# Attention and a routed mixture of experts in one kernel: the end of a batch in fewer VectorE steps at other places, x turned one tile a pair, and a new order of the first and last pairs

## The chip, the cores and the metric

One core of a Trainium2 chip runs the whole program. The metric is device time in microseconds of one execution; lower is better. TensorE (PE) multiplies, VectorE (DVE), ScalarE (ACT) and GpSimd (POOL) do elementwise work, SyncE (SP) starts most transfers.

## The reference, cut to what matters

Attention with a decay, 8 batches of 8 heads, 576 positions of 64 values, and its output `x` (4608 tokens of 512) into a mixture of 8 experts of which each token uses one:

```python
scores = q @ k.T / 8                           # per batch and head, 576 x 576
cum    = cumsum(log(clip(f, 1e-4, 1)))         # decay, per position
scores = where(causal, -1e9, scores + cum[:, None] - cum[None, :])
attn   = exp(scores - max); attn /= sum + 1e-9
x      = (attn @ v)                            # -> 4608 x 512
logits = x @ w_gate                            # 4608 x 8
e      = argmax(logits); g = softmax(logits)[e]
out    = g * (relu(x @ w1[e]) @ w2[e])         # w1 512 x 1024, w2 1024 x 512
```

## The kernel before, in words

**Attention in pairs.** `attention_all` (L183) handles two heads of a batch at a time: 32 pairs, four to a batch, in a loop over n = 0 to 32. The 576 query rows of a head are four tiles of 128 and a short one of 64; the short tiles of both heads are treated together, as "joint rows". In iteration n the scores of pair n are multiplied (L358, joint rows L391), reduced with bias and mask on VectorE (L342, custom operations that add the bias and give the row's largest value), and exponentiated on ScalarE (L377, joint L383). The turned probabilities (64 x 64 turns L410, copied by ScalarE or VectorE at L422; the last rows by L405 and L467) and the products with the values (L481, in two halves AVa and AVb, whose copies to `xT` are `xa` and `xb`) belong to pair n-1.

**What sets the order.** The table `PERIOD` lists each iteration's steps in program order, and `InOrder.pin` makes each engine keep it. Between the steps lie numbered and lettered slots, 0, E, 1, 2, 3, U, X, 4, 5, C, V, F, 6. Slot U is behind VectorE's reduction r12; X is on TensorE between the last turns and the joint rows J; 4 is ahead of the last turns TL and AVa; C is ahead of `xb`; V and F are behind it. Two reductions matter here: `r10` stands behind `tl` (the L467 copy), and the joint reductions `rj0` and `rj1` lie around `xa`.

**Banks.** Turns and products go to seven PSUM banks given out in a cycle (`next_bank`); a bank is free again when its copy has run.

**The end of a batch.** `fin_tasks` (L585) puts tasks into slots of the iterations after a batch's last pair: gate matmuls on TensorE (`fin_gate`, L557), the turning and scaling of x's five row tiles (`fin_x`: turns L410 or L405, products with 1/sum L516 on VectorE, write to DRAM), the logits (`fin_logits`, turns L405, five products L575, sum L581), then the routing of `route_stages` (L819): softmax, expert, gate (L864 to L870), rank (matmuls L875 and L877, sums L882 to L887), slot (L894 to L908), a high one-hot (L912; GpSimd multiplies it by the gate values, L919, Rr), a low one-hot (L926) and the table (matmuls L933, sum L937). Each routing stage is some two to eight VectorE operations on 128 x 5 or 128 x 40; many of their tiles lie in a PSUM bank, `ps_r`. The plan is, as (iterations after, slot): gate matmuls (0, X); x tiles 0 and 1 (0, F); logits (1, X); softmax and expert (1, V); gate (2, U); rank (2, X); slot and high one-hot (2, V); low one-hot (3, U); table (3, X); x tiles 2, 3 (3, F) and 4 (3, C).

**Start and end.** `first_bias` (L248) makes the first pair's bias by products of ones (L255) and copies (L260). q and k are rounded (L293) and what the rounding left is kept as well (`rest`, L298). `selects` (L301) masks a bias tile on GpSimd: joint rows L309, diagonals L314 to L318. In the last pairs expert 0 is begun: three blocks of gathered rows of x are fetched by GpSimd (`fetch`, L1062) in iteration 30, w1's four blocks are loaded and split (L999, L1000), and first up-products run (`up`, L1111), put into slots by the tables of `extra`; `Moe.finish` (L1178) lists the rest of expert 0 and the last batch's routing.

```python
            at("X"), ("J", 0, s_joint), ("r11", 0, most(1, 1)), at(4), ("TL", 1, av_last),
            ("AVa", 1, lambda n: av(n, 0)), ("e11", 0, power(1, 1)), ("tl", 1, out_last),
            ("r10", 0, most(1, 0)), ("e02", 0, power(0, 2)), ("e13", 0, power(1, 3)),
            ("rj0", 0, lambda n: red_joint(n, 0)), ("AVb", 1, lambda n: av(n, 1)), at(5),
            ("xa", 1, lambda n: av_out(n, 0, "v")),
            ("rj1", 0, lambda n: red_joint(n, 1)), ("e12", 0, power(1, 2)), at("C"),
            ("xb", 1, lambda n: av_out(n, 1, "v")), at("V"), at("F"), ("ej", 0, exp_joint), at(6),
```

## Time and profile before

| | us |
|---|---|
| median of 3 runs (lowest, highest) | 800.54 (800.32, 813.82) |
| the profiled execution | 802.31 |
| its span, first to last instruction | 800.6 |
| TensorE busy | 767.2 |
| VectorE busy | 551.1 |
| ScalarE busy | 502.6 |
| GpSimd busy | 500.2 |

The span is the time from the first to the last recorded instruction, and what lies around it in the profiled execution is 1.7 us. The mean granted TensorE clock over the span is 0.981 of full speed. Attention takes about the first 356 us, the experts the rest. How to read it: the chain of waits follows the work that ended last back from the last instruction, and gives for each stretch of time what was running or waited for; the distance between two values products (L481) in that chain is the length of one pair.

### The profile page before, as it was taken

Reading aid. Unit: us, or ns where it says so; the run is one execution under the profiler, and the core shown is the slowest. Engines: PE = TensorE matmul, PEld = TensorE weight load, DVE = VectorE, ACT = ScalarE, POOL = GpSimd, SP = SyncE. Lnnn points to the kernel's source line nnn. Section 1 sums busy time; section 2 is a strip of 40 time slices with the busy share of each in tenths; the row PEclk is TensorE's granted clock in tenths of the full one; section 3 lists DMA queues with packets and bytes.
Section 4 is the critical chain, followed back from the end, with each engine's and each line's share of the span. In section 5 each row is a group of like instructions: output and inputs, shape, how many; then the busy total and the mean of one; then the engine's idle time right before and its main releaser. Section 6 shows DMA issues by size and latency. Waiting matters only on the chain.

```text
span 800.6 us, 18864 instructions
## 1 busy us (share of the span) xinstructions
PE 767.2 (96%) x6640; PEld 640.9 (80%) x6640; DVE 551.1 (69%) x1643; ACT 502.6 (63%) x1276; POOL 500.2 (62%) x620
## 2 busy tenths in 40 slices
PE   5999999999999999989999999999999999999996
PEld 3777776767676767678989899898898898998985
DVE  5668787777888786735388848758478488486630
ACT  5997886887878786755366646456365365463521
POOL 5997685858595957751568657546556475475311
PEclk9999998999999999899999999999999999999999
DMA  7766574847565757421446352363343433523300
GB/s 185 209 170 180 145 218 120 220 135 209 148 206 146 206 149 215 147 89 64 141 110 201 106 165 84 107 197 101 116 144 106 154 93 106 165 74 106 111 26 32
DMA packets 78817, 112.15 MB, mean 140 GB/s; under 512 B 9343, under 2 KB 40063, under 8 KB 78720
## 3 DMA queue, kind: packets, MB, share of 16 engines
q1 hardware_dynamic: 71680, 90.97, 39.6%
q0 software_dynamic: 6400, 19.93, 7.7%
q8 instruction: 54, 0.88, 0.4%
q14 instruction: 43, 0.35, 0.1%
q10 hardware_dynamic: 640, 0.01, 0.0%
HBM read 91.85 MB, written 20.07 MB: 140 GB/s over the span
## 4 chain that ended last, share of the span: by engine, by line
PE 87%; DVE 8%; issue 2%; ACT 1%; DMA 0%; POOL 0%; DVEq 0%; ACTq 0%; POOLq 0%
PE ps L1147 28%; PE ps L1342 19%; PE ps L481 12%; PE ps L358 6%; PE ps L410 6%; PE ps L391 5%; PE ps L1111 4%; DVE sc L342 2%; PE ps L405 2%; PE pr L1342 1%; PE ps L1298 1%; PE ps L557 1%; DVE xT L422 1%; PE pr L933 1%; ACT sc L377 0%
## 5 line engine op out<-in xcount | busy, mean ns | idle before, releaser
L377 ACT ACTIVATE sc<-sc,nmx 128x512 f32<-128x512 f32 (+3 forms) x256 | 142.2, 559 | 24.4 <-DVE nmx L342 24.1
L1147 PE MATMUL ps<-w_0w,hhw 128*128 128x512 f32 x280 | 112.9, 403 | 0.0
L1342 PE MATMUL ps<-X_0w,w1s 128*128 128x320 f32 x504 | 111.7, 309 | 0.0
L422 ACT COPY aT<-ps 128x512 f32<-128x512 f32 (+1 forms) x224 | 94.2, 506 | 27.1 <-PE ps L410 24.2
L1147 PE MATMUL ps<-w_0w,hl 128*128 128x512 f32 x280 | 110.8, 396 | 0.0
L1147 PE MATMUL ps<-w_1w,hhw 128*128 128x512 f32 x280 | 110.4, 394 | 0.0
L1155 POOL DMA_INDIRECT out<-y,si_fast x37 | 37.1, 1004 | 96.8 <-ACT y L1154 88.1
L358 PE MATMUL ps<-hl 64*128 64x512 f32 (+3 forms) x768 | 90.7, 351 | 4.9 <-DVE xT L422 2.6
L481 PE MATMUL ps<-aT,va_t 128*64 128x256 f32 (+3 forms) x896 | 93.7, 361 | 0.3 <-DVE aT L467 0.3
L298 POOL TENSOR_TENSOR hl<-raw,hl 128x512 fp32r<-128x512 f32 (+1 forms) x62 | 83.6, 1349 | 5.0
L1342 PEld LDWEIGHTS ps<-X_0w,w1s 128*128 128x128 f32 x504 | 84.2, 188 | 0.0
L1154 ACT ACTIVATE y<-ps,g_fast 128x512 f32<-128x512 f32 x37 | 25.5, 689 | 87.6 <-PE ps L1147 64.9
L481 PEld LDWEIGHTS ps<-aT,va_t 128*64 128x64 f32 x896 | 57.9, 140 | 27.4 <-issue 2.9
L1342 PE MATMUL ps<-X_1w,w1s 128*128 128x320 f32 x252 | 77.9, 309 | 0.0
L358 PEld LDWEIGHTS ps<-hl 64*128 64x128 f32 x768 | 60.6, 195 | 9.4 <-PE ps L410 3.1
L342 DVE CUSTOM_DVE_ANT_0 sc<-ps,bias 128x128 f32<-128x128 f32 (+1 forms) x128 | 59.2, 481 | 5.8 <-PE ps L358 3.2
L1147 PEld LDWEIGHTS ps<-w_0w,hl 128*128 128x128 f32 x280 | 52.5, 187 | 12.7
L1147 PEld LDWEIGHTS ps<-w_1w,hhw 128*128 128x128 f32 x280 | 52.8, 189 | 11.1
L1389 POOL TENSOR_TENSOR u<-u,u 128x320 f32<-128x320 f32 x27 | 23.6, 876 | 60.7 <-DVE u L1387 60.4
L1147 PEld LDWEIGHTS ps<-w_0w,hhw 128*128 128x128 f32 x280 | 52.5, 188 | 11.0
L342 DVE CUSTOM_DVE_ANT_1 sc<-ps,bias 128x256 f32<-128x256 f32 (+1 forms) x128 | 58.8, 485 | 0.3
L1342 PE MATMUL ps<-xa,w1s 128*128 128x320 f32 x336 | 58.2, 308 | 0.2 <-ACT u L1376 0.2
(241 smaller groups left out, 1886.2 us busy)
## 6 DMA issues: line engine op xcount, KB each, us to landing
bias<-ud SPq DMA_DIRECT2D x31, 576.0 KB
w1r<-in_w SPq DMA_DIRECT2D x112, 128.0 KB
w<-in_w SPq DMA_DIRECT2D x28, 512.0 KB
raw<-in_qkT SPq DMA_DIRECT2D x64, 160.0 KB
raw<-in_qkT SPq DMA_DIRECT2D x64, 144.0 KB
va_t<-in_va SPq DMA_DIRECT2D x32, 256.0 KB
x_dram<-row SPq DMA_DIRECT2D x32, 256.0 KB
wraw<-in_w SPq DMA_DIRECT2D x7, 512.0 KB
```

What stands on the lines that cost most here:

```text
L298: return eng.tensor_tensor(hl[:, 1], raws[n][:, r : r + w], hl[:, 0].bitcast(F32), ALU.subtract)
L342: V.tensor_tensor_reduce(dst, src, in1, -0.125, init, ALU.add, ALU.min, nms[n][:, col : col + 1])
L358: note(nc.tensor.matmul(pb[j][:, o : o + w], hl[js, q, P * t : P * t + P], hl[js, k, 512 : 512 + w], start=(i == 0), stop=(i == 2),))
L377: A.activation(x, x, AF.Exp, bias=nms[n][:, 5 * j + t : 5 * j + t + 1], scale=-1.0, accum_out=ssums[b][:, t, 2 * p + j : 2 * p + j + 1])
L391: note(nc.tensor.matmul(pb[half][64 * j : 64 * j + 64, 0:JW], raw[:, 512 + 64 * j : 576 + 64 * j], raw[:, 640 + JW * half : 640 + JW * hal ...
L410: note(nc.tensor.transpose(out.bitcast(F32R), words, c.identr[rows, rows]))
L422: copy_on = {"a": lambda o, i: A.copy(o, i), "v": lambda o, i: V.tensor_copy(o, i)}
L481: note(nc.tensor.matmul(pv[j * HD : (j + 1) * HD, q0 - qa : qb - qa], l, r, start=(blk == 0), stop=(blk == nb - 1),))
L1111: c.note(nc.tensor.matmul(ph[:, 0:n], w[:, wi, fs], x[xi][:, kt, :], start=(k == 0), stop=(k == 3 * KT - 1),))
L1147: c.note(nc.tensor.matmul(py, rows(hi_, ft), w[wi], start=(ft + k == 0), stop=(ft == FT - 1 and k == 2),))
L1155: nc.gpsimd.indirect_dma_start(out=self.out, out_offset=bass.IndirectOffsetOnAxis(ap=si[:, s : s + 1], axis=0), in_=y, in_offset=None, bou ...
L1342: self.nc.tensor.matmul(bank[:, 0:HN], w[:, wi, mat, kt], x[xi][:, kt, :], start=start and k == 0, stop=k == 5, skip_group_check=True,)
```

## The change

**The batch end.** A tile of x is turned in slot X and written out in slot V, one tile a pair and the last two together (`fin_x` gives two steps; its two half banks are taken at the turning). Logits are turned at X, scaled at 4 with two products in place of five, summed at C. Softmax and expert go to U a pair later, gate to 4 with five of its eight operations on GpSimd, rank to X of the next pair, its sums to 4, slot to C, high one-hot to U, low to C, table to X and its sum to 4 of the pair after. For the batches from 5 on the logits come a pair earlier. The small tiles lie in SBUF instead of `ps_r`; a second subtraction, two memsets, a cast and a sum are dropped. In `PERIOD`, V goes to the place behind `tl`, ahead of `rj0`, and `r10` goes ahead of slot 4.

**The start.** Eleven products of a zero tile run on TensorE ahead of the bias products. `rest` of pair 0 goes ahead of `first_bias`. The second pair's q and k are loaded earlier and rounded ahead of the masks. The joint rows of the first bias are copied from PSUM by ScalarE, and GpSimd masks the diagonals first and then 64 columns of the joint rows alone.

**The end.** The early fetches go from slot 0 to slot 2 of iteration 30, behind the masks of pair 31; w1's blocks are loaded and split in other slots, one of them by ScalarE and VectorE; the first up-products go to slots 3, U, X, 5 and 6 of iteration 32, and `finish` begins with the last batch's logits.

```diff
+        idle = c.words["xT", 0]
+        V.memset(c.values["xT", 1][:, 0:512], 0.0)
+        V.tensor_copy(idle[:, 0:512], c.values["xT", 1][:, 0:512])
+        pi = next_bank()
+        for _ in range(11):
+            note(nc.tensor.matmul(pi, idle[:, 0:P], idle[:, 0:512], start=True, stop=True))
...
+            for c0, w, k in ((512, S - 512, 2), (0, 512, 0)):
+                for j in range(2):
+                    rows = slice(64 * j, 64 * j + 64)
+                    pin(A.copy(biases[0][rows, BJ + c0 : BJ + c0 + w], pb[k + j][rows, 0:w]))
...
+        load_raw(1)
+        for part in (Q, K):
+            pin(rest(0, V, part))
         pin(A.activation(warm, fr[0:1, 0:1], AF.Exp))
         first_bias()
-        for part in (Q, K):
-            pin(rest(0, V, part))
...
-        joint, diagonals = selects(0)
-        joint(384)
+        for part in (K, Q):
+            rounded(1, A.copy, part)
+        diagonals, joint = selects(0)
         diagonals()
-        joint(0, 384)
+        for part in (K, Q):
+            rest(1, G, part)
+        joint()
...
-            at("X"), ("J", 0, s_joint), ("r11", 0, most(1, 1)), at(4), ("TL", 1, av_last),
+            at("X"), ("J", 0, s_joint), ("r11", 0, most(1, 1)),
+            ("r10", 0, most(1, 0)), at(4), ("TL", 1, av_last),
             ("AVa", 1, lambda n: av(n, 0)), ("e11", 0, power(1, 1)), ("tl", 1, out_last),
-            ("r10", 0, most(1, 0)), ("e02", 0, power(0, 2)), ("e13", 0, power(1, 3)),
+            at("V"), ("e02", 0, power(0, 2)), ("e13", 0, power(1, 3)),
...
-            ("xb", 1, lambda n: av_out(n, 1, "v")), at("V"), at("F"), ("ej", 0, exp_joint), at(6),
+            ("xb", 1, lambda n: av_out(n, 1, "v")), at("F"), ("ej", 0, exp_joint), at(6),
...
-            for dn, i, f in [
-                (0, "X", lambda: fin_gate(b)), (0, "F", fx[0]), (0, "F", fx[1]),
-                (1, "X", lg[0]), (1, "X", lg[1]), (1, "V", softmax), (1, "V", expert),
-                (2, "U", gate), (2, "X", rank), (2, "V", slot), (2, "V", hi), (3, "U", lo),
-                (3, "X", table), (3 - 2 * late, "F", fx[2]), (3 - late, "F", fx[3]),
-                (3 - late, "C", fx[4]),
-            ] + after:
+            fx = [fin_x(b, *ts) for ts in ((0,), (1,), (2,), (3, 4))]
+            soon = b >= B - 3
+            k = 1 - soon
+            plan = [(0, "E" if soon else "X", lambda: fin_gate(b))]
+            for i, (f, e) in enumerate(fx):
+                plan += [(i, "X", f), (i, "V", e)]
+            plan += [
+                (k, "X", lg[0]), (k, 4, lg[1]), (k, "C", lg[2]),
+                (k + 1, "U", softmax), (k + 1, "U", expert), (k + 1, 4, gate),
+                (k + 2, "X", rank), (k + 2, 4, ranked), (k + 2, "C", slot),
+                (k + 3, "U", hi), (k + 3, "C", lo),
+            ]
...
+                plan += [(k + 4, "X", table), (k + 4, 4, tabled)]
...
-        w.oh = tokens(80, 6)
-        V.tensor_tensor(w.oh[:, 0:5], bc(w.ei), c.iota5m, ALU.is_equal)
-        V.memset(w.oh[64:128, 4, :], 0.0)
-        V.memset(w.oh[:, 5, :], 0.0)
-        w.ohb = rs.tile([P, 6, E], BF16, name="ohb")
-        V.tensor_copy(w.ohb, w.oh)
+        V.tensor_tensor(c.ohb[:, 0:5], bc(w.ei), c.iota5m, ALU.is_equal)
...
-            V.tensor_copy(vl[:, :, 3 + i], gw)
+            G.tensor_copy(vl[:, :, 3 + i], gw)
             if i < 2:
-                V.tensor_tensor(gw, gw, vl[:, :, 3 + i], ALU.subtract)
+                G.tensor_tensor(gw, gw, vl[:, :, 3 + i], ALU.subtract)
...
-        for kt in range(KT):
+        for kt in (0, 3, 1, 2):
...
-        return [(4, "V", self.early_index)] + [
-            (5, 0, lambda m=m: self.fetch(0, m)) for m in range(NA)
+        return [(4, "C", self.early_index)] + [
+            (5, 2, lambda m=m: self.fetch(0, m)) for m in range(NA)
...
-        return {0: [up(0)], "E": [out, up(1)], 1: [out], 4: [up(2), out],
-                6: [up(3), out, up(4), out]}.get(i, [])
+        return {3: [up(0)], "U": [up(1)], "X": [out], 5: [out], 6: [up(2), out]}.get(i, [])
```

The order of instructions shows it at three places (line, operation, out<-in, shape). First, VectorE in the pair of the gate stage. Before, the stage's eight operations stand between r12, whose largest values are `nmx`, and the copy of turns to `aT`:

```order
L864 TENSOR_REDUCE pr<-ex 128x5
L865 TENSOR_SCALAR pr<-pr 128x5
L866 RECIPROCAL pr<-pr 128x5
L868 CAST vals<-pr 128x5
L870 TENSOR_TENSOR pr<-pr,vals 128x5
L868 CAST vals<-pr 128x5
L870 TENSOR_TENSOR pr<-pr,vals 128x5
L868 CAST vals<-pr 128x5
L422 COPY aT_91<-ps 128x4x64
L342 ISA sc_02_73,nmx<-ps,bias 128x128
L342 ISA nmx 128x1
```

After, the same engine ahead of the last rows' copy (L478) of the pair of the gate stage; L353 is the score reduction:

```order
L353 ISA sc_11_81,nmx<-ps,bias 128x256
L353 ISA nmx 128x1
L353 ISA sc_12_79,nmx<-ps,bias 128x128
L353 ISA nmx 128x1
L908 TENSOR_REDUCE gw<-ex 128x5
L909 TENSOR_SCALAR gw<-gw 128x5
L910 RECIPROCAL gw<-gw 128x5
L478 COPY aT_91<-ps 64x2x64
L533 TENSOR_TENSOR row<-ps,rinv 128x4x64 x2
```

The gate stage is three operations here, in slot 4, and the writing of x (L533, `row`) stands directly behind the L478 copy.

Second, VectorE in the pair that has the slot stage, from the last rows' copy's surroundings on. Before, around both output copies to `xT`, the joint reductions (`sc_J`) come first and the slot stage behind the second copy:

```order
L342 ISA sc_J,nmx<-ps,bias,nmx 128x288
L342 ISA nmx 128x1
L422 COPY xT_83<-ps 128x256
L894 TENSOR_REDUCE r<-rk 128x5
L895 SCALAR_TENSOR_TENSOR key<-pr,r 128x5
L899 TENSOR_TENSOR th<-pr,iotaP 128x20
L904 TENSOR_REDUCE hi<-th 128x5
L906 SCALAR_TENSOR_TENSOR pr<-hi,pr 128x5
L908 SCALAR_TENSOR_TENSOR pr<-pr,hi 128x5
L912 TENSOR_TENSOR eqh<-pr,iotah 128x200
L722 MEMSET ssum 64x8
L342 ISA sc_03_57,nmx<-ps,bias 128x512
```

After, where two tiles of x are written in the same pair:

```order
L478 COPY aT_97<-ps 64x2x64
L533 TENSOR_TENSOR row<-ps,rinv 128x4x64 x2
L533 TENSOR_TENSOR row<-ps,rinv 64x4x64 x2
L353 ISA sc_J,nmx<-ps,bias 128x288
L353 ISA nmx 128x1
L433 COPY xT_83<-ps 128x320
L353 ISA sc_J,nmx<-ps,bias,nmx 128x288
L353 ISA nmx 128x1
L936 SCALAR_TENSOR_TENSOR key<-ei,rkp 128x5
L940 TENSOR_TENSOR th<-rkp,iotaP 128x20
L945 TENSOR_REDUCE hi<-th 128x5
L947 SCALAR_TENSOR_TENSOR lo<-hi,rkp 128x5
```

The four writes stand ahead of the first joint reduction, and the slot stage between the second joint reduction and the second output copy.

Third, GpSimd in iteration 30. Before, the rows of x are fetched (`xg`) and a weight block is split ahead of the mask of the last pair's `bias`:

```order
L298 TENSOR_TENSOR hl<-raw,hl 128x576
L1062 DMA xg<-x_dram,gi_early 128x512 x3
L999 CAST w_6344<-wraw 128x1024
L1000 TENSOR_TENSOR w_6344<-wraw,w_6344 128x1024
L309 AFFINE_SELECT bias<-bias 64x576 x2
L314 AFFINE_SELECT bias<-bias 128x2x128
L316 AFFINE_SELECT bias<-bias 128x2x192
L318 AFFINE_SELECT bias<-bias 128x2x256
L1000 TENSOR_TENSOR w_6462<-wraw,w_6462 128x1024
```

After, the mask stands ahead of the fetch:

```order
L308 TENSOR_TENSOR hl<-raw,hl 128x576
L319 AFFINE_SELECT bias<-bias 64x576 x2
L325 AFFINE_SELECT bias<-bias 128x2x128
L327 AFFINE_SELECT bias<-bias 128x2x192
L329 AFFINE_SELECT bias<-bias 128x2x256
L1105 DMA xg<-x_dram,gi_early 128x512 x3
L912 CAST vals<-gw 128x5
L914 TENSOR_TENSOR gw<-gw,vals 128x5
L912 CAST vals<-gw 128x5
```

The fetches, and the splitting of the weight block, moved behind the four mask rows; the gate stage's GpSimd rows (`vals`, `gw`) follow the fetches.

## Rows read from the trace of the kernel before

**Rows 1.** The first page: busy time of each engine (share of the span, instructions), and the chain of work that ended last, by engine.
```profile
PE 767.2 (96%) x6640; PEld 640.9 (80%) x6640; DVE 551.1 (69%) x1643; ACT 502.6 (63%) x1276; POOL 500.2 (62%) x620
...
PE 87%; DVE 8%; issue 2%; ACT 1%; DMA 0%; POOL 0%; DVEq 0%; ACTq 0%; POOLq 0%
```

**Rows 2.** The chain of waits (start us, us, what) in the stretch from 41 to 52 us, which has no batch end: the values products of two pairs that follow each other.
```profile
41.93 2.87 PE ps L481 x32
...
50.24 1.77 PE ps L481 x17
```

**Rows 3.** Busy time by windows (window: length, then busy us and instructions of PE, PEld, DVE, ACT, POOL, the granted TensorE clock as a share of 2.4 GHz, DMA share, GB/s): ten us of plain pairs, three stretches of the first batches, two whole batches, and a stretch of the last pairs.
```profile
30.00:40.00 10.00, 10.00 (x153) 8.15 (x151) 7.33 (x30) 9.58 (x29) 9.42 (x20) 1.00 0.75 197
77.00:80.40 3.40, 3.17 (x25) 1.79 (x21) 2.70 (x17) 2.20 (x7) 0.00 (x1) 0.50 0.03 11
118.00:124.80 6.80, 6.80 (x51) 4.51 (x52) 4.66 (x28) 5.35 (x16) 1.41 (x1) 0.50 0.31 84
162.70:165.80 3.10, 2.88 (x20) 1.48 (x18) 2.45 (x15) 1.89 (x7) 0.16 (x1) 0.51 0.06 20
187.10:269.10 82.00, 77.54 (x1042) 59.59 (x1042) 66.09 (x286) 66.67 (x207) 59.89 (x89) 1.00 0.61 179
343.40:346.70 3.30, 3.23 (x10) 3.23 (x11) 0.68 (x3) 0.00 (x0) 2.27 (x5) 0.51 0.21 79
```

**Rows 4.** The chain of waits (start us, us, what) through one batch in the middle: five values products, and between them pieces of TensorE and VectorE.
```profile
187.08 2.87 PE ps L481 x32
...
192.74 1.28 PE ps L410 x32
...
194.75 0.55 PE ps L405 x5
...
196.60 2.92 PE ps L481 x32
...
203.90 0.13 DVE pr L864
...
205.55 0.18 PE pr L875
...
205.84 1.12 PE ps L391 x8
...
207.14 2.89 PE ps L481 x32
...
214.31 0.75 DVE Ar L926
...
215.10 0.69 PE pr L933 x5
...
217.09 2.87 PE ps L481 x32
...
225.72 1.11 PE ps L557 x16
...
228.12 2.87 PE ps L481 x32
```

**Rows 5.** VectorE's groups in that batch (201.1 to 242.15 us), shapes of one line together: line, operation, out<-in, shapes, count | busy us, mean ns | idle before.
```profile
L516 DVE TENSOR_TENSOR row<-ps,rinv 128x256 f32<-128x256 f32 (+1 forms) x9 | 3.5, 442 | 1.2 <-PE ps L405 1.2
...
L467 DVE COPY aT<-ps 64x128 f32<-64x128 f32 x4 | 1.1, 280 | 1.3 <-PE ps L405 1.3
...
L887 DVE TENSOR_REDUCE pr<-rk 128x5 f32<-128x40 f32 x1 | 0.2, 203 | 0.0
...
L894 DVE TENSOR_REDUCE r<-rk 128x5 f32<-128x40 f32 x1 | 0.2, 185 | 0.0
```

**Rows 6.** GpSimd's groups in the same stretch, same columns.
```profile
L919 POOL TENSOR_TENSOR Rr<-eqh,vals 128x240 bf16<-128x240 bf16 x5 | 2.8, 586 | 6.8 <-DVE eqh L912 6.8
```

**Rows 7.** The chain of waits in the stretch from 78 to 81 us: the joint rows of pair 6.
```profile
78.42 2.12 PE ps L391 x8
```

**Rows 8.** VectorE's timeline at the start (start us, us, line, operation, out<-in, count, in brackets the idle time before it and what ended it).
```profile
9.69 1.49 DVE L298 TENSOR_TENSOR hl<-raw,hl 128x512 fp32r<-128x512 f32 x2
...
12.63 0.69 DVE L342 CUSTOM_DVE_ANT_0 sc<-ps,bias 128x512 f32<-128x512 f32 x1 [1.33 <-PE ps L358]
...
18.89 0.69 DVE L342 CUSTOM_DVE_ANT_0 sc<-ps,bias 128x512 f32<-128x512 f32 x1 [1.83 <-POOL bias L314]
```

**Rows 9.** GpSimd's timeline at the start, same columns.
```profile
9.68 1.71 POOL L309 TENSOR_SCALAR_AFFINE_SELECT bias<-bias 64x192 f32<-64x192 f32 x2 [7.13 <-ACT bias L260]
```

**Rows 10.** The chain of waits over the last pairs: the values products of pairs 29 to 31 (written in the next pair's steps) and the last one.
```profile
310.19 2.89 PE ps L481 x32
...
323.04 4.45 PE ps L481 x32
...
337.13 2.87 PE ps L481 x32
...
355.93 1.96 PE ps L481 x20
```

**Rows 11.** GpSimd's timeline in the last pairs: the first of three early fetches of rows of x, and the mask of the last pair.
```profile
315.69 1.22 POOL L1062 DMA_INDIRECT xg<-x_dram,gi_early  x1 [4.29 <-DVE row L516]
...
322.85 1.39 POOL L309 TENSOR_SCALAR_AFFINE_SELECT bias<-bias 64x576 f32<-64x576 f32 x2
```

**Rows 12.** TensorE's waits from 300 to 360 us (its line <- the engine, tile and line waited for: us in total, times, longest).
```profile
PE ps L1111 <- DVE xa L1082: 1.5, 1, 1.5
```

More of the change, by code (lines that the diff above doesn't have):

```diff
@@ L320, in diagonals @@
                                 channel_multiplier=1)
-            return joint, diagonals
+            return (joint, diagonals) if n else (diagonals, lambda: joint(512))
         def added(n, j, t):
@@ L583, in attention_all @@
         tasks, later, order = {}, [], InOrder(tc)
         def fin_tasks(b):
-            (softmax, expert, gate, rank, slot, hi, lo, table), after = batch_done(
-                b, lambda: lgs[b][0], next_bank
-            )
-            fx = [lambda t=t: fin_x(b, t) for t in range(5)]
-            lg = [lambda p=p: fin_logits(b, p) for p in range(2)]
+            (softmax, expert, gate, rank, ranked, slot, hi, lo, table, tabled), after = batch_done(
+                b, lambda: lgs[b], next_bank
+            )
@@ L695, in prepare @@
                 load_bias(n + 2)
-            if n == 0 and i == 0:
+            if n == 0 and i == 2:
                 late_consts()
-                for part in (Q, K):
-                    rounded(1, A.copy, part)
-                for part in (Q, K):
-                    rest(1, G, part)
             if n + 1 < NP and i == 1:
@@ L730, in behind @@
                 todo = fin_tasks(b - 1)
-            for f in tasks.pop((n, i), []):
-                step(f)
             if n >= NPAIR:
@@ L739, in behind @@
                     fin_sums(b - 1, part)
+            for f in tasks.pop((n, i), []):
+                step(f)
             if (n, i) == (NP, 0):
@@ L822, in route_stages @@
     V = nc.vector
+    G = V if last else nc.gpsimd
     rs = c.rps
```

221 lines of the change are left out of this document (122 added, 99 removed).

## Prediction

> **What bounds the kernel now.** I read the first page, then the chain of waits pair by pair, then the busy time by windows, then VectorE's groups. TensorE is busy 96% of the 800.6 us span and carries 87% of the chain that ended last; VectorE carries 8% of the chain though it is busy only 69% [rows 1]. So time can be won only where TensorE stands, or turns at half speed, and those places are few.
>
> The ruler is the distance from one pair's values products (L481) to the next. Plain pairs, with no batch-end work, come every 8.31 us (41.93 to 50.24) [rows 2]; in them TensorE is busy 10.00 of 10 us and ScalarE 9.58, so ScalarE is nearly a second bound there [rows 3]. A batch in the middle takes 41.04 us (187.08 to 228.12), in steps of 9.52, 10.54, 9.95 and 11.03 [rows 4]. Four plain pairs are 33.24. TensorE's own batch-end work is: gate 1.11, table 0.69, logits turns 0.55, the rank 0.29 (205.55 to 205.84), and the turns of x. Thirty-two half turns took 1.28, so one is 0.04 and the 32 of x's four full tiles cost 1.28; four whole turns for the short tile are 0.44 by 0.55 for five [rows 4]. The sum is 4.36. So the work is 33.24 + 4.36 = 37.6, and 3.4 us of each batch are waits. The busy time bounds that from the other side: 77.54 of 82.00 us over two batches leaves 2.2 a batch [rows 3].
>
> Where the 3.4 are: take each step, less 8.31 and its own work. Step 1 has logits and two tiles of x (0.55 + 0.64): 0.0 left. Step 2 has the rank: 10.54 - 8.31 - 0.29 = 1.9 left. It is the gate chain: eight small VectorE operations from 203.90 to 205.5, behind which the rank waits, and the joint rows (L391) stand behind the rank on TensorE [rows 4]. Step 3 has the table: 0.95 left, the slot chain and, from 214.31, the low one-hot L926, for which the table at 215.10 waits [rows 4]. Step 4 has gate, two tiles and the short tile: 11.03 - 8.31 - 1.11 - 1.08 = 0.5 left.
>
> **The change in the batch.** TensorE's work stays 4.36; only its place moves. On VectorE the small operations cost about 0.2 us each: 185 ns for one sum over 40, 203 for another [rows 5]. Counting the order rows, a batch end had some 46 VectorE operations and has some 33: five of the gate's eight go to GpSimd, one subtraction, two memsets, a cast and a sum are dropped, the logits' five multiplications become two. That is 13 x 0.19 = 2.5 us less VectorE time a batch. This alone is worth nothing where VectorE is idle. What counts is order:
>
> - The softmax stands where the gate chain stood, but its rank comes a pair later, so nothing stands behind it on TensorE. The 1.9 us of step 2 go.
> - The table comes a pair after the low one-hot, and its sum on VectorE is a slot of its own: the 0.95 of step 3 go.
> - New: the writing out of x (two of 442 ns a tile) stands between the last turns' copy and the first joint reduction, no longer behind the second output copy. Banks go round in sevens. In the logits' pair, the first values product gets the bank that this write must free, and it is asked for before the copy. It then waits for the copy (0.28) and one write (0.44): 0.7 [rows 5].
> - New: the exponential of the softmax sits in ScalarE's queue and waits for two small VectorE operations (0.2 each) and then takes about as long itself, an estimate. Behind it are copies that free banks for the joint rows. ScalarE has 0.4 us of slack in 10 [rows 3], so most shows: 0.5, at most 0.9.
> - New: with the short tile, four writes (1.8 us) and the slot chain (four small ones, 0.8) stand ahead of the second output copy, which the next pair's second group needs a bank from: 0.6.
> - With some 0.3 for the half-microsecond waits that stay, new and old waits are 0.7 + 0.5 + 0.6 + 0.3 = 2.1 where 3.4 were. The batch becomes 39.7: 1.35 us less. Bounds: no new wait shows (-3.4), or the new ones are double (+0.6).
>
> Five GpSimd operations more a batch are hidden: GpSimd stands idle 6.8 us before Rr in that batch anyway [rows 6], and its other work there is for pairs to come. If that cover went, they would cost about 1 us.
>
> Six batch ends lie in the steady stretch: 6 x 1.35 = 8.1 us.
>
> **The clock.** [...] One stretch so costs 1.0 us (at most 1.7, if all of the 3.4 were work); four cost 4.3. With shorter waits some won't come. I can't tell which: I take 2 of 4.3, with 0 and 4.3 as ends.
>
> **The start.** Rounding's remainder of the first pair, 1.49 us for two on VectorE from 9.69, held the first scores until 11.2; it moves ahead of the bias copies, where VectorE stands waiting for the bias products [rows 8]. GpSimd's joint mask (1.71 at 9.68) moves behind the diagonals, so the first score reduction, at 12.63 after a wait of 1.33 for TensorE, can go at about 11.3 [rows 8, 9]. The second pair's reduction at 18.89 had waited 1.83 for a mask on GpSimd [rows 8]; that mask comes about as much earlier, as the joint mask of pair 0 shrinks. Together 1.3 to 2.3 of the path, and I take 2.0. The eleven products of zeros run before 6.8, when TensorE has nothing; they cost nothing if they end by then. By the joint rows' 0.14 to 0.27 us for 288 columns one of 512 is 0.25 to 0.47 (an estimate), eleven are 2.7 to 5.2 us from about 2 on: at the long end they push the bias products back by half a microsecond. Ends: -3 and 0.
>
> **The end.** Here three pairs took 12.85, 14.09 and 18.80 us (310.19, 323.04, 337.13, 355.93) [rows 10]. Ahead of the last mask on GpSimd stood the early fetches, the first of which waited until 315.69, so that the mask began at 322.85 [rows 11]; now it is first and can begin near 311, so that pair 31's reductions stop waiting. The fetch comes after it at little loss: its rows are turned from the end of that pair on. The up-products at 343.4 ran at half clock behind a 1.5 us wait for xa [rows 3, 12]; they now stand later, spread over four slots. Against that, the copy of one w1 block moves to ScalarE and its subtraction to VectorE, where a pair without a batch end leaves room. I take 12.85 to 11.1, 14.09 to 11.5 and 18.80 to 17.2: 1.75 + 2.6 + 1.6 = 6.0; ends 2 (only the mask's step) and 9.
>
> The sum is 8.1 + 2 + 2 + 6 = 18.1. The profiled execution took 802.31 us (1.7 around its span), the median of the runs is 800.54, so I count from the median: 800.5 - 18.1 = 782.4, say **782 us**.
>
> [...] Two rows differ in where the result goes: a sum over 40 into SBUF took 185 ns, the like into PSUM 203 [rows 5]. So moving the small tiles out of PSUM saves some 18 ns an operation, 16 operations, 0.3 us a batch, which I left out. [...]
>
> **Rivals.**
> - *The waits only move.* The values product waits for the write of x, ScalarE for the softmax, and the batch stays near 41. For it: ScalarE's 9.58 of 10 [rows 3], and VectorE's steps in the joint stretch are packed. Against: the gate chain's 1.9 us is the one long wait, and it has no like afterwards. Then only start, end and a little clock remain: 2 + 6 + 1, so 791 us.
> - *All waits go.* No new wait shows: 6 x 3.4 = 20.4, clock 4.3, start 2, end 8: 35 less, 766 us. Against: three named waits each have a queue behind them.
> [...]
> - *It doesn't do what it says* at the ends: the zeros delay the bias products and the fetch comes late for its turns. 8 less is won: 790, within the first rival's range.
>
> **How the numbers follow.** Forecast 0.56 (its own range 777 to 788), waits only move or ends fail 0.30, all waits go 0.09, clock oftener 0.05. The range of 8 in 10 cuts the last two partly: 772 to 794. A change of 2%, 16 us, is about what a measurement of this kernel can tell from none, so faster means below 784.5: seven tenths of the forecast's 0.56 (0.39), all of 0.09, and a tenth of 0.30, with the unknown end's luck 0.55; slower than 816.5 only the worst of the last rival and what I have not seen, 0.04; the rest, 0.41, is the same.
>
> **What would show it.** Right: values products of a middle batch 39.7 us apart over four pairs, the step of the rank under 9.5, no VectorE chain ahead of L391, the chain's share of VectorE below 8%, first scores near 9, last pairs near 11, 11.5 and 17. Wrong: TensorE waiting over 1 us a batch for the write of x or for copies behind the softmax's exponential; half-clock stretches in every batch; the first score reduction still after 12 us; the last pairs as long as before.

## The result, and the profile after

| | before | changed |
|---|---|---|
| median of 4 runs, us | 800.43 | 778.99 |
| lowest and highest | 796.13, 813.82 | 777.24, 780.01 |
| profiled execution: span, mean granted clock | 800.6, 0.981 | 778.2, 0.987 |

The ratio is 0.9747, with a 95% interval of 0.9701 to 0.9793: faster by 2.5%. The forecast was 782 us. Runs of a kernel that took over 1.5% longer than its fastest one at a lower granted clock are left out of every ratio, but not of the medians.

The first page after, busy times and the chain by engine:

```profile
PE 756.6 (97%) x6679; PEld 639.5 (82%) x6679; DVE 545.5 (70%) x1546; ACT 504.5 (65%) x1280; POOL 508.0 (65%) x655
...
PE 88%; DVE 5%; ACT 3%; issue 2%; POOL 1%; DMA 1%; SPq 0%; ACTq 0%; POOLq 0%; DVEq 0%
```

Against [rows 1], TensorE's share rose to 97%, and VectorE's part of the chain fell from 8% to 5%. VectorE's busy time fell by only 5.6 us (551.1 to 545.5), where eight batches of the forecast 2.5 us would be 20; the last section shows why. So VectorE's total doesn't explain the gain; what it is made of, the runs below take apart.

The chain of waits through one batch in the middle (start us, us, what; L492 are the values products, L973 the table, L416 whole turns, L919 the rank, L402 the joint rows, L421 half turns, L891 the softmax's subtraction):

```profile
135.68 2.87 PE ps L492 x32
...
142.67 0.62 PE pr L973 x5
...
143.72 0.55 PE ps L416 x5
...
145.59 0.74 issue
146.33 2.94 PE ps L492 x32
...
152.72 0.21 DVE sh L891
...
152.96 0.02 ACT ex L895
...
153.10 1.40 ACT aT L433 x4
...
155.43 2.87 PE ps L492 x32
...
162.43 0.53 PE ps L421 x16
162.95 0.13 PE pr L919
...
163.19 1.12 PE ps L402 x8
...
164.49 2.87 PE ps L492 x32
...
174.47 2.87 PE ps L492 x32
```

The batch takes 38.79 us (135.68 to 174.47) where 41.04 were [rows 4], in steps of 10.65, 9.10, 9.06 and 9.98. The rank at 162.95 runs without a wait, and the joint rows follow at once. Two waits are new, and both were foretold: 0.74 us of "issue" at 145.59, ahead of the values products in the logits' step, and the softmax's exponential at 152.96, which starts only when VectorE's subtraction (L891, to 152.93) is done, with four copies of ScalarE (1.40) behind it, for which the joint rows wait.

Values products over the last pairs, those of [rows 10]:

```profile
293.41 2.94 PE ps L492 x32
...
302.68 2.87 PE ps L492 x32
...
314.02 2.94 PE ps L492 x32
...
329.85 2.87 PE ps L492 x32
```

The three steps are 9.27, 11.34 and 15.83 us. Before, they were 12.85, 14.09 and 17.4. The last of these is not the 18.80 of the prediction: the row at 355.93 in [rows 10] has 20 of the pair's 32 products, and TensorE's timeline of before shows the first twelve earlier:

```profile
354.46 1.20 PE L481 MATMUL ps<-aT,va_t 128*64 128x320 f32 x12
355.93 1.84 PE L481 MATMUL ps<-aT,va_t 128*64 128x256 f32 x16 [0.27 <-DVE aT L467]
```

So the chain's distance is the length of a pair only between rows that both hold all 32; from here on, steps go by a pair's first product.

Windows (length, busy us and instructions of PE, PEld, DVE, ACT, POOL, granted TensorE clock, DMA share, GB/s; the clock, here as in [rows 3], is a share of full speed, and no run shows what full speed is in GHz): the start, the 240 us of batches, and the stretch at half clock in the last pairs:

```profile
10.00:16.00 6.00, 5.76 (x31) 4.10 (x33) 4.23 (x20) 4.97 (x13) 3.84 (x7) 0.50 0.93 199
50.00:290.00 240.00, 235.35 (x3248) 182.26 (x3245) 196.98 (x792) 207.97 (x639) 199.26 (x310) 1.00 0.70 188
320.60:327.40 6.80, 6.00 (x42) 5.83 (x43) 3.31 (x9) 3.25 (x10) 4.63 (x8) 0.51 0.49 135
```

Between 50 and 290 us the granted clock is 1.00 throughout, where before had four stretches of 3.4 us at half clock [rows 3]. At the start it's the other way: from 10 to 16 us the changed kernel runs at 0.50.

**Where the time went, by the two traces.** To the fifth pair's values products: 59.65 to 58.42 us, 1.2 less. Over the next 24 pairs: 250.5 to 235.0, 15.5 less. The three steps of the end: 44.3 to 36.4, 8.0 less. From there to the end of the span, where the experts are: 446.1 to 448.4, 2.3 more. The sum is 22.4, as the spans differ. The last two belong together: 36 matmuls of the first up-products stood ahead of the last values products before, 24 do now, and twelve take 2.4 us. And the 8.0 hang on the clock: a second profile of the changed kernel has 40.2 us for those three steps, with two stretches of 6.8 us at half clock where the first has one.

### The profile page after: what moved, and what is told of

It reads as the page before. It is cut to its first block, busy times and chain, and to the rows that moved or that the text cites. A ratio compares the mean times of both kernels' runs of the same rounds, so it can differ in the third digit from the quotient of the medians.

```text
span 778.2 us, 18921 instructions
## 1 busy us (share of the span) xinstructions
PE 756.6 (97%) x6679; PEld 639.5 (82%) x6679; DVE 545.5 (70%) x1546; ACT 504.5 (65%) x1280; POOL 508.0 (65%) x655
## 4 chain that ended last, share of the span: by engine, by line
PE 88%; DVE 5%; ACT 3%; issue 2%; POOL 1%; DMA 1%; SPq 0%; ACTq 0%; POOLq 0%; DVEq 0%
PE ps L1190 27%; PE ps L1386 18%; PE ps L492 12%; PE ps L369 9%; PE ps L421 8%; PE ps L402 5%; PE ps L1154 3%; PE ps L416 1%; PE pr L1386 1%; PE ps L1342 1%; PE ps L587 1%; ACT aT L433 1%; DVE sc L353 1%; DVE w1s L1291 1%; PE pr L973 1%
## 5 line engine op out<-in xcount | busy, mean ns | idle before, releaser
L1198 POOL DMA_INDIRECT out<-y,si_fast x37 | 37.3, 1007 | 95.0 <-ACT y L1197 86.5
L492 PE MATMUL ps<-aT,va_t 128*64 128x256 f32 (+3 forms) x896 | 90.7, 353 | 5.6 <-PE ps L416 5.5
L369 PE MATMUL ps<-hl 64*128 64x512 f32 (+3 forms) x768 | 88.1, 346 | 0.8 <-ACT bias L264 0.8
L308 POOL TENSOR_TENSOR hl<-raw,hl 128x576 fp32r<-128x576 f32 (+1 forms) x62 | 83.8, 1352 | 5.8 <-ACT hl L303 0.8
L492 PEld LDWEIGHTS ps<-aT,va_t 128*64 128x64 f32 x896 | 58.5, 137 | 29.8 <-PE ps L416 6.6
L353 DVE CUSTOM_DVE_ANT_0 sc<-ps,bias 128x128 f32<-128x128 f32 (+1 forms) x128 | 59.7, 485 | 13.6 <-PE ps L369 9.4
L369 PEld LDWEIGHTS ps<-hl 64*128 64x128 f32 x768 | 58.1, 190 | 5.7 <-ACT bias L264 1.2
L1190 PEld LDWEIGHTS ps<-w_1w,hhw 128*128 128x128 f32 x280 | 52.6, 188 | 10.2
L353 DVE CUSTOM_DVE_ANT_1 sc<-ps,bias 128x256 f32<-128x256 f32 (+1 forms) x128 | 57.6, 487 | 3.5 <-PE ps L369 3.5
```

What stands on the lines that cost most here:

```text
L308: return eng.tensor_tensor(hl[:, 1], raws[n][:, r : r + w], hl[:, 0].bitcast(F32), ALU.subtract)
L353: V.tensor_tensor_reduce(dst, src, in1, -0.125, init, ALU.add, ALU.min, nms[n][:, col : col + 1])
L369: note(nc.tensor.matmul(pb[j][:, o : o + w], hl[js, q, P * t : P * t + P], hl[js, k, 512 : 512 + w], start=(i == 0), stop=(i == 2),))
L492: note(nc.tensor.matmul(pv[j * HD : (j + 1) * HD, q0 - qa : qb - qa], l, r, start=(blk == 0), stop=(blk == nb - 1),))
L1190: c.note(nc.tensor.matmul(py, rows(hi_, ft), w[wi], start=(ft + k == 0), stop=(ft == FT - 1 and k == 2),))
L1198: nc.gpsimd.indirect_dma_start(out=self.out, out_offset=bass.IndirectOffsetOnAxis(ap=si[:, s : s + 1], axis=0), in_=y, in_offset=None, bou ...
```

## The experiments

All times are medians; ratios are to the kernel before, run beside each on the same chip, where its medians were 805 to 807 us. The gate tile, the gate in slot 4, no zeros and logits first were run on one chip, all others on a second, so between those two groups ratios are compared, not times. The mean granted clock differs from run to run, so the column "us at equal clock" takes that out: over the 33 runs of before that the ratios take in, the span fits 788.6 us plus 663 us times (1 - mean granted clock) to within about 1 us, and the column says how far a kernel's runs lie from that line, less what before's own runs beside them do (its error is 0.2 to 0.9 us).

| run | us | ratio (95%) | us at equal clock | batches, us: least, median | granted clock 50 to 290 us |
|---|---|---|---|---|---|
| gate tile in SBUF, else before | 804.1 | 1.003 (0.998 to 1.008) | -2.8 | 41.1, 43.3 | 0.95 |
| gate in slot 4, else before | 806.1 | 1.010 (1.005 to 1.014) | +1.8 | 42.1, 42.1 | 0.95 |
| fewer steps alone | 803.4 | 0.996 (0.991 to 1.001) | -5.4 | 40.1, 41.9 | 0.95 |
| other places alone | 810.7 | 1.011 (1.008 to 1.015) | +6.0 | 41.0, 42.3 | 0.99 |
| five gate steps back on VectorE | 802.2 | 1.001 (0.997 to 1.005) | -1.3 | 40.3, 41.5 | 0.99 |
| no zeros | 778.5 | 0.974 (0.967 to 0.981) | -16.6 | 38.1, 38.8 | 1.00 |
| logits first | 777.0 | 0.972 (0.965 to 0.979) | -19.3 | 38.2, 38.7 | 1.00 |
| logits first, exponential late | 783.1 | 0.973 (0.968 to 0.978) | -17.7 | 37.3, 38.5 | 1.00 |
| fetches first | 782.9 | 0.973 (0.968 to 0.978) | -15.9 | 38.1, 39.1 | 1.00 |
| changed, again | 783.4 | 0.978 (0.973 to 0.982) | -16.2 | 38.6, 38.9 | 1.00 |
| logits first, no zeros | 779.1 | 0.972 (0.968 to 0.976) | -19.1 | 37.8, 38.6 | 1.00 |
| the same, exponential late in early batches | 780.6 | 0.973 (0.968 to 0.977) | -19.0 | 37.6, 38.5 | 1.00 |

The batches are the six between the fifth and the 29th values products of the profile; in before their least is 41.03 and their median 41.6, in the changed kernel's first profile 38.5 and 38.8. The last two columns are of one profile each (before's has 0.97), and a median takes in half-clock stretches.

The theory behind the prediction was that the gate's chain stood ahead of the rank on TensorE, and that placing was what counted. The rivals: the wait came from a tile that two stages share (A), or the two crowded pairs are bounded by VectorE's work as such (C).

**The wait alone.** In before, the rank's matmuls wait for the gate because both write the PSUM tile `ps_r`. One line takes that away:

```diff
-        gw = part(136, 5)
+        gw = rs.tile([P, 5], F32, name="gw")
```

> The kernel before with one edit: the gate stage's sum (gw) is a tile in SBUF instead of columns of the PSUM tile ps_r that the rank's matmuls write too. Order on every engine as before. Theory A (false wait): the rank waits for the gate chain only because both write ps_r; so the step of the rank falls from 10.54 to 9.0 to 9.4 us, the half-clock stretches behind that wait mostly go, and the time falls by 8 to 15 us, to 785 to 792. Theory B (order): the eight operations stand ahead of the last turns' copy on VectorE, and the joint rows wait for a bank that this copy frees; the step stays above 10.2 and the time within 3 us of 800.

The ratio is 1.003, so no gain shows in it; at equal clock the kernel is 2.8 us shorter. The chain of waits in the step of the rank (L875) of an undisturbed batch, where L467 is the copy of the last rows:

```profile
122.25 0.13 PE pr L875
...
122.49 0.66 PE ps L391 x4
123.15 0.40 DVE aT L422
...
124.26 0.21 DVE rk L885
...
125.17 0.21 DVE aT L467
...
125.42 1.98 PE ps L481 x20
```

The rank now starts without a wait, and the joint rows after it. But four of their eight are done when the copy of the last turns (123.15), still behind the gate's eight operations on VectorE, becomes what is late; the reductions and the rank's sums (124.26) push the last rows' copy to 125.17, and the second half of the values products waits for it. The steps of 9.52 and 10.54 with the next 9.95 [rows 4] became 9.53, 9.89 and 10.66: the sum is the same (the row at 125.42 has the second part of the pair's products).

But this edit is two edits. The tile also moved from PSUM to SBUF, and there the second of the gate's eight operations takes four times as long, in this run and then in before (line, count | busy us, mean ns | idle before):

```profile
L865 DVE TENSOR_SCALAR gw<-gw 128x5 f32<-128x5 f32 x6 | 4.2, 705 | 0.2
```

```profile
L865 DVE TENSOR_SCALAR pr<-pr 128x5 f32<-128x5 f32 x6 | 1.0, 171 | 0.2
```

That is 0.53 us more on the same chain, about as much as the wait that went. Theory A as it was put, 8 to 15 us, is out even so: the 2.8 us and six times 0.53 are 6.0, or 1.0 a batch (an estimate from these rows). What the wait costs by itself isn't shown; the tile in PSUM columns of its own was not run.

**The place of the gate alone.** `(2, "U", gate), (2, "X", rank)` became `(2, "X", rank), (2, 4, gate)`.

> The kernel before with one edit: the gate stage goes from slot U to slot 4 of the same pair, behind the rank, its tile still in PSUM, all eight operations on VectorE. Theory A and B both say that the joint rows no longer wait for it; the 1.6 us chain now delays the copy of the last rows and what follows. A: the step of the rank is 9.0 to 9.6 and the time 785 to 792, as in the run with the tile in SBUF. B: it is clearly faster than that run, by 5 us or more.

The ratio is 1.010, and 1.8 us more at equal clock: no gain, with the tile still in PSUM. The eight operations, now ahead of the last rows' copy, held the values products for 1.4 us in the one batch that had no half-clock stretch (42.08 us). So my account of the 1.9 us (the order on TensorE) also fails: with the rank's wait taken away, neither kernel is faster by anything like 1.9 us a batch.

**Fewer steps alone, and other places alone.** The first is the kernel before with the shorter stages and logits in the old slots; the second is the changed kernel, its start and end included, with all the dropped work put back. Both have the small tiles in SBUF. From the first one's edit:

```diff
-        V.tensor_tensor(w.oh[:, 0:5], bc(w.ei), c.iota5m, ALU.is_equal)
-        V.memset(w.oh[64:128, 4, :], 0.0)
...
-            V.tensor_copy(vl[:, :, 3 + i], gw)
+            G.tensor_copy(vl[:, :, 3 + i], gw)
```

> The kernel before, with the changed kernel's shorter routing stages and logits (some 13 VectorE operations fewer a batch end, five of the gate's on GpSimd, small tiles in SBUF), all in the slots of before; x, the table of steps, start and end as before. Theory C (VectorE's work in the two crowded pairs is what bounds them): the undisturbed batch falls from 41.0 to 39 to 40 us and the time to 784 to 792. Theory D (placing is what counts: the stages still stand in the pairs where joint reductions and copies are due): the batch stays above 40.3 and the time above 793.

> The changed kernel with the dropped work put back where its stages now stand: the gate's five operations on VectorE, the second subtraction, two memsets, the cast, the second sum, and five products for the logits. Slots, x, start and end as changed. Theory C: the 2.5 us of VectorE work a batch come back to a good part, the batch goes from 38.8 to 39.8 to 41 us, the time to 785 to 794. Theory D: they fall into VectorE's gaps, the batch stays under 39.4 and the time at 779 to 783.

Fewer steps alone leave a ratio of 0.996, inside its error, and are 5.4 us shorter at equal clock. The values products of its last undisturbed batch:

```profile
271.45 2.87 PE ps L481 x32
...
311.57 1.55 PE ps L481 x15
```

40.12 us, 0.9 below 41.04, and six times that is the 5.4. The window of the batches (columns as above) shows a granted clock of 0.95 in this profile:

```profile
50.00:290.00 240.00, 230.54 (x2982) 174.52 (x2981) 185.70 (x732) 192.79 (x593) 183.60 (x287) 0.95 0.63 174
```

That is this one execution: over all twelve runs the mean granted clock of the whole span is 0.974, over the 23 of before beside them 0.975. Other places alone are slower than before, 1.011 and 6.0 us at equal clock: the steady batch is 40.96 (10.74, 9.12, 11.07, 10.02; the third, which holds the second part of the products behind the gate, was 9.06), so nothing of the 2.2 us is left, and from the 25th values products to the last, where the batch ends crowd, it takes 88.9 us against 76.1. My range for it, 785 to 794, left those pairs out. Neither half does it; together they give 2.2 us a batch. That is neither C nor D as I put them: the saved work is worth 0.9 us a batch in the old slots, and the new slots are good only with the saved work. One thing is not separated: in the second run the work put back in slot 4 may itself have been slow (with the gate's five operations alone back there, a cast took 365 ns on average against 176 in before; see the last section). The new slots with the old work and its tiles in PSUM were not run.

**Which of the work.** The changed kernel with one edit, the gate's five operations back on VectorE, in slot 4:

```diff
-            G.tensor_copy(vl[:, :, 3 + i], gw)
+            V.tensor_copy(vl[:, :, 3 + i], gw)
...
-                G.tensor_tensor(gw, gw, vl[:, :, 3 + i], ALU.subtract)
+                V.tensor_tensor(gw, gw, vl[:, :, 3 + i], ALU.subtract)
```

> The changed kernel with one edit: the gate's five operations behind its reciprocal run on VectorE again, in the same slot 4; all other savings stay. Theory E (slot 4 lies ahead of the copy of the last rows, and the second half of the values products waits for that copy): of the 2.2 us that the run with all work put back lost in a batch, 1.0 to 1.8 come back with these five alone, the pair of the softmax goes from 9.1 to 10.1 to 10.9, and the time to 786 to 797. Rival (the loss came from the eight other operations, ahead of the last turns' copy): the pair stays under 9.6 and the time under 783.

802.2, ratio 1.001, and of 16.2 us at equal clock 1.3 are left: these five take nearly the whole gain back, 11.9 us over the 20 pairs up to the 25th values products (207.3 against 195.4) and 9.9 from there to the last (86.0 against 76.1). TensorE's waits from 48 to 290 us (line, what it waited for: total, times, longest):

```profile
PE ps L492 <- DVE aT L478: 11.5, 6, 2.2
PE ps L492 <- PE ps L416: 4.2, 6, 1.0
```

The second line is the 0.74 us wait that the changed kernel has too:

```profile
PE ps L492 <- PE ps L416: 4.0, 5, 1.0
```

The first line is new: six times, once a batch, the values products wait up to 2.2 us for the last rows' copy L478. VectorE's timeline there shows why (start, length), with a mask on GpSimd (POOL) below:

```profile
160.30 0.47 DVE L912 CAST vals<-gw 128x5 bf16<-128x5 f32 x1
...
161.78 0.58 DVE L912 CAST vals<-gw 128x5 bf16<-128x5 f32 x1
162.26 0.27 DVE L478 COPY aT<-ps 64x128 f32<-64x128 f32 x1
```

```profile
161.69 0.63 POOL L329 TENSOR_SCALAR_AFFINE_SELECT bias<-bias 128x512 f32<-128x512 f32 x1
```

The copy starts at 162.26 because the gate's chain ends then. These casts take 0.47 and 0.58 us where they took 0.174 in before; the second begins inside the mask and ends with it, and the last section comes to that. So theory E stands, larger than expected: what pays is that slot 4 holds three gate operations, not eight. By first products the pair of the softmax keeps its 9 us or so, and the next grows from 9.1 or 9.3 to between 11.1 and 11.4 in three of the first four batches (12.7 in the one with a half-clock stretch), since it is the second part of the products that waits. How much is the number of the operations and how much their slowness is open: over the six batches the gate's scalar operation, casts and subtractions take 6.3 us longer than at the durations of before, beside 11.5 us of waits. Eight of them at those durations in slot 4, all else as changed, were not run.

**The new waits.** Turning the logits ahead of the tile of x gives the first values product a bank that is free early:

> The changed kernel with one edit: in the pair that has both, the logits are turned ahead of the tile of x, so that the first values product gets the bank that the logits' scaling frees, and not the one that the writing of x frees. Theory (bank wait): the wait of 0.74 us ahead of the values product in each batch goes, pairs of 10.65 us become 9.9, and the time falls by 3.5 to 5 us, to 774 to 775.5. Rival (the wait is for the copy of the last rows, or comes back a step later): no change, 779.

The logits' steps fall from 10.7 to 9.7, as expected, and the next ones grow from 9.0 to between 9.1 and 9.8. Of the first four batches two are as long as before that edit, and two 0.3 and 0.6 shorter. The chain in such a pair (L492 are values products):

```profile
145.15 2.87 PE ps L492 x32
...
151.69 0.02 ACT ex L895
...
151.84 1.40 ACT aT L433 x4
...
155.42 1.96 PE ps L492 x20
```

The pair now waits for the softmax's exponential at 151.69 and the copies behind it, as in the changed kernel; much of what it comes to earlier, it waits for longer. So I moved that too:

> The changed kernel with the logits turned first, as in the run before, and the softmax's exponential moved from slot U to slot X (behind the copies that free the joint rows' banks), the gate from 4 to C. Theory (the exponential's wait in ScalarE's queue costs the pair of the softmax 0.45 us): that pair goes from 9.1 to 9.6 down to 8.7 to 9.1, three microseconds in all, to 773 to 775. Rival (ScalarE's own load is the bound there and the wait only moves): 776 to 778, as with the logits first alone.

In two of the first four batches the pair of the softmax does fall, from 9.8 and 9.7 to 8.6 and 8.8 us, but the pair two steps on grows from 10.0 to between 10.2 and 10.4, and the 24 pairs take 231.5 us against 232.3 with the logits first alone: 0.8 less where three were expected, so the rival held. The time, 783.1, is of the second chip, on which the changed kernel itself took 783.4. In its profile the last three steps take 43.3 us, with three stretches at half clock in them, 20 us in all. Whether the gate's later place brought these on wasn't settled. Keeping the move to the early batches:

> The run without zeros and with the logits first, and with the softmax's exponential at X and the gate at C for the first five batches alone, since in the last ones the gate at C kept GpSimd from the masks. Theory: 0.2 us a batch less than without that move, 774 to 776. Rival: no difference from it.

780.6 against 779.1 without it, and no shorter batches: the rival held again.

Turning the logits first is worth something by itself, if less than the 3.5 to 5 us expected: over the 24 pairs the four profiles with it have 231.5 to 232.3 us, the four without it, the rest of the batch end as changed, 234.3 to 235.1.

**The start.** Without the eleven products of zeros:

> The changed kernel without the eleven products of zeros at the start. Theory (the products raise the clock early or cost nothing): the first values product comes at 23.7 to 25.5 us and the time is 779 to 781. Rival (the products bring on the half-clock stretch that the changed kernel shows from 10.0 to 16.8 us, in which scores and joint rows take twice as long): the first values product comes at 21.5 to 23 us and the time is 776.5 to 778.

778.5, with the first values product at 22.2 against 23.7. The window of that start:

```profile
10.00:16.00 6.00, 6.00 (x42) 4.16 (x40) 4.29 (x20) 4.96 (x14) 4.98 (x8) 1.00 0.94 194
```

Full clock, where the changed kernel had 0.50. Over all profiles: of seven with the zeros five have a stretch at half clock that begins at 10 to 11 us, of three without none; one that begins at 19 to 21 us is in all seven and in two of the three. The first values products come at 22.5 to 24.0 us with them and at 22.2 to 23.9 without. So the zeros bring no earlier start; more half clock goes with them in these ten profiles, too few to be sure. That they cost time is not shown.

**The end.** The fetches ahead of the mask, `(5, 2, ...)` back to `(5, 0, ...)`:

> The changed kernel with the three early fetches back in slot 0 of iteration 30, ahead of the last pair's masks on GpSimd. Theory (the mask behind the fetches held the last pair's reductions): the last values product comes 2 to 5 us later than at 329.9, the time is 781 to 784. Rival (the fetches no longer wait long, or the end of the tail is set by the experts' first products): 778 to 780.

GpSimd's timeline of the changed kernel (L319 is the mask, L1105 the fetch), and then of this run:

```profile
292.35 1.39 POOL L319 TENSOR_SCALAR_AFFINE_SELECT bias<-bias 64x576 f32<-64x576 f32 x2
...
296.14 1.23 POOL L1105 DMA_INDIRECT xg<-x_dram,gi_early  x1 [0.85 <-DVE pr L1019]
```

```profile
297.56 1.23 POOL L1105 DMA_INDIRECT xg<-x_dram,gi_early  x1 [3.74 <-DVE pr L1019]
...
301.31 0.68 POOL L319 TENSOR_SCALAR_AFFINE_SELECT bias<-bias 64x576 f32<-64x576 f32 x1
304.25 0.67 POOL L319 TENSOR_SCALAR_AFFINE_SELECT bias<-bias 64x576 f32<-64x576 f32 x1 [2.27 <-DMA xg<-x_dram,gi_early]
```

The mask's first half moves from 292.35 to 301.31, 9 us later (1.4 of them because this run came to the pair that late), and its second half waits another 2.27 us for the fetches' data. The three last steps take 40.2 us against 36.4, as expected, but the changed kernel's own second profile also has 40.2, and the ratio, 0.973, is none the worse. What the mask's place is worth stays open.

**The best version, beside the changed kernel on the same chip:**

> The changed kernel once more, beside the next three on the same chip: 777 to 780, as measured; the span against the granted clock of each run gives the line on which the others are compared.

> The changed kernel with the logits turned first and without the products of zeros. By the two single runs (0.5 and 2 us less in the median, at equal clock 0 and 1.5 to 2 less): 775 to 777, 2 to 3 below the changed kernel on this chip. Rival (both differences were the clock of those runs): equal to the changed kernel within 1 us.

The changed kernel missed its 777 to 780 on this chip; its ratio there, 0.978, leaves open whether it is faster by 2%. The best version has 779.1 against 783.4, in ratios 0.972 (0.968 to 0.976) and 0.978 (0.973 to 0.982). The intervals overlap a little; at equal granted clock (0.989 and 0.990) the spans are 776.4 to 777.7 and 778.3 to 781.8. It is the best version beside the changed kernel on one chip, by 2 to 4 us.

## Why the prediction was right, and where only by luck

**The sum.** Forecast 18.1 less, measured 21.4 in the medians and 22.4 between the profiles. By its terms:

- *The batch*: 8.1 forecast. The 24 pairs are 15.5 shorter. Four half-clock stretches of before are in that: its three disturbed batches were 42.07, 43.30 and 42.06 long against 41.04, so 4.3. The rest is 11.2, or 1.9 a batch where 1.35 stood. The step that was mis-sized is that of the new waits: 0.7 and 0.5 were right (0.74; and 9.10 - 8.31 - 0.32 = 0.47), but the 0.6 for the short tile did not come (step three, 9.06, is 8.31 and its own 0.29 and 0.53 to within 0.1).
- *The clock*: 2 forecast with 0 and 4.3 as ends; it was 4.3, the whole. Before's granted clock was 0.50 from 77.0 to 80.4 and from 118.0 to 124.8 us, and 0.51 from 162.7 to 165.8 [rows 3], four stretches of some 3.4 us; in the first, eight joint rows took 2.12 us [rows 7] against the 1.12 at 205.84 [rows 4], so one costs about 1.0 us (an estimate from these two rows).
- *The start*: 2.0 forecast; 1.65 at the fourth pair, 1.2 at the fifth.
- *The end*: 6.0 forecast; 8.0 less 2.3 is 5.7 by the first profile, and about 2 by the second. The steps were right only in sum: the 18.80 was misread and was 17.4, I had not counted that an up-product goes behind the last values products, and the fetches' place, on which I leaned, isn't shown to matter.

**The step that failed** is "nothing stands behind it on TensorE. The 1.9 us of step 2 go." The time came out, the reason did not. With the rank's wait gone and all else as before at most 1.0 us a batch came of it, with the chain elsewhere in the pair nothing. In before TensorE's timeline records a shorter wait for the gate in that step, with 0.52 us for ScalarE ahead of it:

```profile
205.55 0.18 PE L875 MATMUL pr<-ohb,trib 128*128 128x48 bf16 x1 [0.59 <-DVE vals L868]
```

That is 0.59 us, not 1.9. In both runs VectorE was late over the crowded pairs, and with one link taken out of its chain the next one waited. The five operations on GpSimd, which I priced at 0.2 us each and called "worth nothing where VectorE is idle", decide: behind the new place stands the last rows' copy, for which TensorE waits (11.5 us in six waits with the five back on VectorE), and VectorE is not idle in slot 4.

**The rivals.** *The waits only move* is what happens to the gate's place, the other places and the exponential by themselves, and to most of the gate tile's wait; fewer steps alone keep 0.9 us a batch. It wasn't so for the whole. *All waits go* was nearer than I thought: of 3.4 us of waits 1.2 stay. That the clock falls oftener, in the chances *clock oftener*, did not happen in the changed kernel: from 50 to 290 us it has 1.00, before 0.97. Nor is it shown of the edits to before: the 0.95 of their profiles against 0.97 is one execution each, and over all their runs the mean granted clock is 0.975 and 0.977, of before beside them 0.976.

**The clock, as far as it goes.** Before's line is 788.6 us plus 663 us times (1 - mean granted clock); over ten runs of the changed kernel it is 771.8 plus 664 times. So at the same clock, 0.98, 801.9 and 785.1: 16.8 us are the change itself, and the rest of the difference, some 5 us, is that its clock falls less (0.988 on average over those ten, 0.975 over all 64 runs of before beside the experiments). What brings the falls isn't settled. They aren't simply the longest waits: the run with the gate's five operations has six waits up to 2.2 us and one fall in 240 us, while before has waits of at most 0.7 and four. In before those four come in the pair of the rank, from 77.0, 118.0 and 162.3 us, and in each of the three pairs TensorE had stood 0.52 us for ScalarE shortly ahead (at 74.72, 116.78 and 160.08); but the undisturbed batch of [rows 4] has that wait of 0.52 us too (at 202.15), and no fall. Filling the wait with other products wasn't tried.

## What to carry to other kernels

A wait that the profile names is the last link of a chain; before pricing it at its length, ask what on the same engine is late next, and put the work of the whole crowded stretch against its time. Fewer instructions and better places can be worth little or less than nothing each, and far more together (here, at equal clock, 5.4 us less, 6.0 more, and 16.2 less together): test both halves, and then the few instructions that stand right ahead of a copy which another engine needs. An edit that takes a wait away by moving a tile to another memory is two edits, and wants a run for each. And a term that comes out right may hide two wrong ones; the sum over the steps must be checked step by step.

## What the runs showed of the hardware

With small tiles in SBUF in place of PSUM, some VectorE operations became slower, where I had expected them 18 ns shorter. Groups of the changed kernel from 48 to 293 us (count | busy us, mean ns | idle before):

```profile
L951 DVE SCALAR_TENSOR_TENSOR hj<-ei,hi 128x5 f32<-128x5 f32 x6 | 3.2, 528 | 0.0
L936 DVE SCALAR_TENSOR_TENSOR key<-ei,rkp 128x5 f32<-128x5 f32 x6 | 3.0, 503 | 0.0
...
L898 DVE SCALAR_TENSOR_TENSOR cand<-sh,iota5c 128x40 f32<-128x40 f32 x6 | 2.6, 436 | 0.2
```

and the same three stages in before, where one operand lies in PSUM:

```profile
L849 DVE SCALAR_TENSOR_TENSOR cand<-pr,iota5m 128x40 f32<-128x40 f32 x6 | 1.1, 189 | 0.0
...
L895 DVE SCALAR_TENSOR_TENSOR key<-pr,r 128x5 f32<-128x5 f32 x6 | 1.0, 165 | 0.2
L908 DVE SCALAR_TENSOR_TENSOR pr<-pr,hi 128x5 f32<-128x5 f32 x5 | 0.9, 172 | 0.2
```

528, 503 and 436 ns against 172, 165 and 189. In the changed kernel the eight `key` operations range from 149 to 645 ns, in before from 163 to 166. Their time went with what GpSimd was doing. Of all runs of these three lines and of L903 in the changed kernel, 18 began while a GpSimd instruction was under way, and each ended 0.01 to 0.06 us after that instruction ended: the `key` of 645 ns began at 206.06 us and ended at 206.70, and the two masks that GpSimd had begun at 205.30 ended at 206.69. The other 14 took 149 to 202 ns; two of them are the `key` that met an idle GpSimd, with 149 and 164 ns. With the same tiles and the five gate operations back on VectorE, `key` took 241 and `hj` 226 on average, while `cand` took 440. So in these rows the time goes with what GpSimd is doing when such an operation begins, not with the memory as such: undisturbed, the gate's scalar operation took 172 ns in the changed kernel and 171 in before, and the 18 ns of the prediction don't show there. Other operations on SBUF tiles fared in two ways. Sums and the minimum kept their time, also beside GpSimd (the minimum over experts, L902, 196 to 197 ns; the sum L945, six times beside a mask, 175 to 177, where before's L904 took 176). Casts and the scalar operation did not: the 0.58 us cast above, the 705 ns in the first edit, and in the changed kernel the one scalar operation that began beside a GpSimd instruction, at 349.63 us, which took 1.36 us and ended 0.02 us after it. By the rows the three lines cost 0.36 + 0.34 + 0.25 = 0.9 us more of VectorE a batch than in before, which the prediction did not weigh, and no run here gave it back. With the gate's five operations back on VectorE the casts and subtractions took 365 and 310 ns on average where they took 176 and 171 in before.
